# Sending all of the first 21 slots' attention-weight transposes through TensorE and dropping its warm-ups in the loop, in an attention and MoE kernel

## The chip, the cores and the metric

The kernel runs on one core of one Trainium2 chip. The metric is the device time of one execution in microseconds (us), lower is better. Times are medians of several executions.

Engines are named as in the profile: PE is TensorE, PEld its weight loads, DVE VectorE, ACT ScalarE, POOL GpSimd, SP SyncE (it issues the loads, the stores and the DMA crossbar's transposes). The *granted clock* is the share of its full clock that PE was given: in the records of these traces it is 1.00 or 0.5 (half clock).

## The reference, cut to what matters

```python
# q, k, v: (8, 8, 576, 64) float32; tau = 0.02
scores = q @ k.T / sqrt(64)
thresh = max(scores, axis=-1) - tau
attn   = softmax(where(scores >= thresh, scores, -1e9))
x      = (attn @ v)            # to (4608, 512)
h      = x @ w_in              # (512, 2048)
out    = (h * clip(h + 3, 0, 6) / 6) @ w_out
```

## The kernel before

The work is cut into 144 *slots*: one slot is the softmax of 128 queries of two heads against 576 keys. Nine slots make a quad (four heads). In the first 22 slots (`N1`) there is no projection work yet, because no attention output is complete. After that the projections of batch b run beside the softmax of the next batches. The attention weights of a slot, `pn`, have queries in the partitions; the product with v needs keys there, so each slot's `pn` is transposed into `pT` (or `pR` for a quad's ninth slot). There are two ways:

```python
def sm_norm(sl):                      # POOL: pn = s * rinv, bf16
    ...
    if not sl.on_chip:                # way 1: the DMA crossbar, straight into SBUF
        nc.sync.dma_start_transpose(out=sl.dst, in_=pn[...])

def pe_transpose(sl):                 # way 2: nine PE transposes into ps_h, the projections' banks
    ps = ps_h.tile([P, 2, 1024], BF16, tag="h", name="pt")
    for c in range(9):
        nc.tensor.transpose(ps[:, c, :], pn[:, c * P:(c + 1) * P], identb[:])
    return lambda: nc.vector.tensor_copy(out=sl.dst, in_=ps)      # and one DVE copy out
```

The loop of slots, cut. Every engine executes its instructions in this order:

```python
for n, sl in enumerate(queue):
    sm_exp(prev)                      # ACT, two activations
    sm_max(sl)                        # DVE: row maxima of this slot; POOL: bias from them
    ...                               # projections, from slot 23
    copies = pe_transpose(queue[n - 2]) if n > 1 and queue[n - 2].on_chip else None   # PE
    sm_recip(prev)                    # DVE
    if copies:
        copies()                      # DVE
    ...
    sm_mask(sl)                       # ACT, two activations, wait for POOL's bias
    ...                               # PE: transposes of q or k, or products with v; DVE: their eviction
    queue[n + 1].tiles = scores(...)  # PE, eight matmuls
    if n < 8:
        warm_up(6)                    # PE: six idle transposes
    sm_norm(prev)                     # POOL
    start(loads, 1)                   # SP: q and k
    if n < 4 or n > 12:
        start(vcasts, 1)              # POOL issues: v
    if n > 3:
        start(casts, 1 if n < 24 else 2)   # POOL issues: w_in, w_out
```

## Time and profile before

| | before |
|---|---|
| time, median of 3 | 562.35 us (562.04 to 563.1) |
| profiled span | 562.3 us |
| busy: PE, DVE, ACT, POOL | 95%, 75%, 84%, 54% |
| slot 2's to slot 22's first mask | 18.23 to 79.11 us: 60.88 us, 3.04 us a slot |
| crossbar transposes | 119 to `pT`, 15 to `pR` |

I read the stage that the change touches by the *first mask* of each slot: the start of its first mask activation on ACT in the timeline. ACT is the fullest engine there, and masks come once a slot, so these times show at which slot time is gained or lost.

### The profile page before, as it was taken

Reading aid. Unit: us, or ns where it says so; the run is one execution under the profiler, and the core shown is the slowest. Engines: PE = TensorE matmul, PEld = TensorE weight load, DVE = VectorE, ACT = ScalarE, POOL = GpSimd, SP = SyncE. Lnnn points to the kernel's source line nnn. Section 1 sums busy time; section 2 is a strip of 40 time slices with the busy share of each in tenths; the row PEclk is TensorE's granted clock in tenths of the full one; section 3 lists DMA queues with packets and bytes.
Section 4 is the critical chain, followed back from the end, with each engine's and each line's share of the span. In section 5 each row is a group of like instructions: output and inputs, shape, how many; then the busy total and the mean of one; then the engine's idle time right before and its main releaser. Section 6 shows DMA issues by size and latency. Waiting matters only on the chain.

```text
span 562.3 us, 11634 instructions
## 1 busy us (share of the span) xinstructions
PE 535.0 (95%) x3856; PEld 309.3 (55%) x3856; DVE 424.4 (75%) x1040; ACT 470.3 (84%) x999; POOL 305.2 (54%) x646
## 2 busy tenths in 40 slices
PE   7998798899999999999999999999999999999997
PEld 5665455455545565555555565655555565654663
DVE  3588787687878788787878798887978798883440
ACT  4799899798988999989898999899898999983540
POOL 1678878854556555655456555755556555561000
PEclk8899999899999999999999999999999999999999
DMA  5879999997689876978589867987699865453102
GB/s 110 135 110 166 162 160 184 207 148 144 112 159 153 151 153 127 208 139 155 114 150 170 159 137 146 174 160 146 127 137 175 167 124 117 101 109 86 38 20 75
DMA packets 286204, 77.52 MB, mean 138 GB/s; under 512 B 269248, under 2 KB 281536, under 8 KB 286144
## 3 DMA queue, kind: packets, MB, share of 16 engines
q1 hardware_dynamic: 268736, 67.86, 64.8%
q0 software_dynamic: 17408, 8.92, 13.7%
q8 instruction: 30, 0.49, 0.4%
q14 instruction: 30, 0.25, 0.2%
HBM read 36.70 MB, written 9.44 MB: 82 GB/s over the span
## 4 chain that ended last, share of the span: by engine, by line
PE 58%; DVE 11%; ACT 9%; issue 4%; POOL 1%; DMA 1%; SPq 1%; DVEq 0%; POOLq 0%
PE h L353 18%; PE o L382 17%; PE s L256 16%; DVE s L277 5%; ACT s L285 4%; PE av L323 3%; ACT s L290 3%; DVE g L370 2%; DVE r L364 2%; ACT r L362 2%; PE s L262 1%; PE tp L213 1%; PE ar L323 1%; DVE osb L390 1%; POOL pn L298 1%
## 5 line engine op out<-in xcount | busy, mean ns | idle before, releaser
L298 POOL TENSOR_SCALAR pn<-s,rinv 128x576 bf16<-128x576 f32 x288 | 211.6, 745 | 133.5 <-issue 58.5
L277 DVE TENSOR_SCALAR_CACHE_REDUCE s<-s 128x576 f32<-128x576 f32 x288 | 205.9, 752 | 44.9 <-PE s L256 35.2
L285 ACT ACTIVATE s<-s,bias 128x576 f32<-128x576 f32 x288 | 207.1, 766 | 36.8 <-POOL bias L280 35.7
L290 ACT ACTIVATE s<-s 128x576 f32<-128x576 f32 x288 | 192.7, 671 | 0.3
L256 PE MATMUL s<-kT,qT 64*128 64x288 f32 x1024 | 172.7, 435 | 5.4 <-DVE s L277 3.2
L353 PE MATMUL h<-xT,w_in_sb 128*128 128x320 bf16 (+1 forms) x1024 | 145.0, 287 | 5.5 <-DVE g L370 4.6
L382 PE MATMUL o<-w_out_sb,g 128*128 128x512 bf16 x576 | 140.9, 379 | 3.6 <-DVE osb L390 3.0
L353 PEld LDWEIGHTS <-w_in_sb 128*128 128x128 bf16 x1024 | 92.0, 97 | 68.4 <-issue 31.1
L256 PEld LDWEIGHTS s<-kT,qT 64*128 64x128 f32 x1024 | 94.8, 188 | 62.7 <-DVE s L277 24.9
L370 DVE SCALAR_TENSOR_TENSOR g<-r,h 128x512 bf16<-128x512 f32 (+1 forms) x128 | 96.4, 754 | 41.2 <-ACT r L362 39.3
L280 POOL TENSOR_SCALAR bias<-m 128x1 f32<-128x1 f32 x288 | 54.4, 189 | 69.0 <-DVE s L277 48.2
L382 PEld LDWEIGHTS <-g 128*128 128x128 bf16 x576 | 55.6, 98 | 58.2 <-issue 9.8
L362 ACT ACTIVATE r<-h,three 128x640 f32<-128x640 f32 (+1 forms) x74 | 54.4, 737 | 21.1 <-PE h L353 20.4
L290 ACT ACTIVATION_READ_ACCUMULATOR s<-s 128x1 f32 x288 | 54.2, 188 | 0.0
L364 DVE TENSOR_SCALAR r<-h 128x512 f32<-128x512 f32 (+1 forms) x54 | 40.5, 751 | 0.0
L390 DVE TENSOR_SCALAR osb<-o 128x512 f32<-128x512 f32 x31 | 21.0, 676 | 22.2 <-PE o L382 22.2
L323 PE MATMUL av<-pT,vm 128*64 128x512 bf16 x256 | 34.6, 392 | 2.0 <-ACT kT L203 2.0
L323 PEld LDWEIGHTS <-vm 128*64 128x64 bf16 x512 | 18.1, 111 | 25.2 <-issue 18.3
L293 DVE RECIPROCAL rinv<-rsum 128x2 f32<-128x2 f32 x144 | 23.0, 160 | 10.2 <-ACT s L290 9.5
L335 DVE CAST xT<-av 128x512 bf16<-128x512 f32 x32 | 21.8, 681 | 5.6 <-PE av L326 5.3
L277 DVE DVE_READ_ACCUMULATOR s<-s 128x1 f32 x288 | 23.9, 83 | 0.0
L388 ACT ACTIVATE osb<-o 128x512 f32<-128x512 f32 x5 | 3.0, 597 | 23.9 <-PE o L382 23.9
(42 smaller groups left out, 255.9 us busy)
## 6 DMA issues: line engine op xcount, KB each, us to landing
km<-in_k_dram SPq DMA_DIRECT2D x64, 128.0 KB, 3.0
out_dram<-osb SPq DMA_DIRECT2D x32, 256.0 KB, 2.4
nq<-in_q_dram SPq DMA_DIRECT2D x96, 72.0 KB, 2.7
vm<-in_v_dram POOLq DMA_DIRECT2D x16, 256.0 KB, 5.4
nq<-in_q_dram SPq DMA_DIRECT2D x16, 128.0 KB, 3.9
w_in_sb<-in_moe_w_in_dram POOLq DMA_DIRECT2D x16, 128.0 KB, 4.1
w_out_sb<-in_moe_w_out_dram POOLq DMA_DIRECT2D x16, 128.0 KB, 4.5
pT<-pn SPq DMA_TRANSPOSE x119, 3.4
```

Source lines behind the costliest of these rows:

```text
L256: nc.tensor.matmul(tiles[a][:, hf, 0:HALF], qT_of(pair)[a * 64:(a + 1) * 64, t * P:(t + 1) * P], keys(pair, a, hf), start=True, stop=True)
L277: nc.vector.tensor_scalar(out=sl.s[:, i, :].rearrange("p (a b) -> p a b", a=2), in0=ps[:, :, 0:HALF], scalar1=1.0, scalar2=None, op0=Alu.m ...
L280: nc.gpsimd.tensor_scalar(out=sl.bias[:, i:i + 1], in0=sl.m[:, i:i + 1], scalar1=-scale, scalar2=tau, op0=Alu.mult, op1=Alu.add)
L285: nc.scalar.activation(out=s, in_=s, func=Act.Prelu, bias=sl.bias[:, i:i + 1], scale=scale, alpha=REJECT)
L290: nc.scalar.activation(out=s, in_=s, func=Act.Exp, accum_out=sl.rsum[:, i:i + 1])
L298: nc.gpsimd.tensor_scalar(out=pn[:, i, :], in0=sl.s[:, i, :], scalar1=sl.rinv[:, i:i + 1], scalar2=1.0, op0=Alu.mult, op1=Alu.mult)
L323: nc.tensor.matmul(ps[a * 64:(a + 1) * 64, :], vm[:, 2 * hp + a, c * D:(c + 1) * D], pT[:, 5 * a + c, cols], start=(c == 0), stop=False)
L353: nc.tensor.matmul(hps[:, n, 0:w], w_in_sb[:, ki, (ni + n) * P:(ni + n + 1) * P], xT[b][:, ki, c0:c0 + w], start=(ki == 0), stop=(ki == KI ...
L362: nc.scalar.activation(out=r, in_=hps, func=Act.Relu, bias=three[:])
L364: nc.vector.tensor_scalar(out=r, in0=hps, scalar1=3.0, scalar2=0.0, op0=Alu.add, op1=Alu.max)
L370: nc.vector.scalar_tensor_tensor(out=gbuf[:, ni:ni + 2, c0:c0 + w], in0=r, scalar=6.0, in1=hps, op0=Alu.min, op1=Alu.mult)
L382: nc.tensor.matmul(o_ps[0], gbuf[:, ni, mt * P:(mt + 1) * P], w_out_sb[:, ni, :], start=(ni == 0), stop=(ni == NI - 1))
```

## The change

Its intent: PE's banks for the projections (`ps_h`) are idle for the first 22 slots, so let all of the first 21 slots use them, and take eleven crossbar transposes off the DMA queue. As PE now has work in every slot, the warm-ups in the loop go.

```diff
-            sl.on_chip = len(queue) < N1 - 1 and len(queue) % 2 == 1
+            sl.on_chip = len(queue) < N1 - 1
...
-        if n < 8:
-            warm_up(6)
```

## The prediction

> **What bounds the kernel now.** I began with the page's busy shares and its 40 slices. PE is the engine of the whole (95% busy), and from about 120 us until the end its digits are all 9. The change acts before that: the 22 slots (a slot is one softmax step of two heads by 576 keys) that run before the first projection matmuls. So I asked for the busy time of each engine in stretches, whose columns are stretch, length, then busy us of PE, PEld, DVE, ACT and POOL, the granted clock, DMA share and GB/s.
>
> ```profile
> 0.00:20.00 20.00, 16.75 (x78) 11.49 (x79) 7.08 (x22) 9.82 (x19) 6.00 (x18) 0.83 0.54 101
> 20.00:40.00 20.00, 18.54 (x153) 12.27 (x152) 15.53 (x43) 17.66 (x40) 15.34 (x33) 1.00 0.82 127
> 40.00:60.00 20.00, 17.51 (x132) 10.24 (x133) 16.79 (x46) 18.34 (x39) 17.50 (x37) 1.00 1.13 166
> 60.00:80.00 20.00, 16.44 (x137) 8.90 (x136) 15.38 (x44) 18.26 (x42) 16.46 (x36) 1.00 1.21 171
> ```
>
> In this stage ACT is fullest (about 18.3 of 20 us), PE, DVE and POOL are each at 15 to 18: no engine is a clear bound. The timeline of ACT gives the pace. Between the first mask of slot 2 (18.23 us) and of slot 22 (79.11) lie 60.88 us, 3.04 us a slot. Where ACT never waits (45.87 to 48.61) a slot takes 2.74. Twenty slots at 2.74 would be 54.8, so about 6.1 us are lost to waits, and the waits of ACT in that stretch say the same:
>
> ```profile
> ACT s L285 <- POOL bias L280: 6.7, 13, 1.6
> ```
>
> 6.7 us in 13 waits, all for the tiny bias, which POOL makes from the row maximum of DVE, which needs PE's scores. The loop is PE scores, DVE maximum, POOL bias, ACT mask and exponential, DVE reciprocal, POOL normalise, then transpose. Two places stand out in the DMA issues and timelines. In slots 14 to 17 POOL itself is the pace (two weight or V loads issued per slot; slots of 3.38, 3.25, 3.26 and, where it ends, 2.67 us). At the start it is PE: the timeline of PE shows
>
> ```profile
> 10.46 2.96 PE L256 MATMUL s<-kT,qT 64*128 64x288 f32 x8 [0.39 <-DVE s L277]
> 13.35 1.54 PE L164 MATMUL warm<-identf 128*128 128x128 f32 x6
> 14.82 2.29 PE L256 MATMUL s<-kT,qT 64*128 64x288 f32 x8
> 17.04 1.20 PE L164 MATMUL warm<-identf 128*128 128x128 f32 x6
> ```
>
> and the timeline of DVE, where the maximum of slot 2 waits for those scores:
>
> ```profile
> 17.14 0.76 DVE L277 TENSOR_SCALAR_CACHE_REDUCE s<-s 128x576 f32<-128x576 f32 x1 [2.84 <-PE s L256]
> ```
>
> Here the warm-ups (six idle transposes after each of the first eight slots) stand between two groups of scores, on the path.
>
> **What the Trainium skill says.** (1) VectorE: DVE Perf Modes, "The three transpose paths": TensorE transposes a full 128x128 bf16 tile in 390 ns but only into PSUM, the DMA crossbar in 1309 ns straight into SBUF. The trace agrees in kind: a PE transpose lasts 219 ns here and nine pipelined ones 0.66 us, a crossbar transpose of a whole slot 3.4 us from issue to landing; the PSUM result costs a DVE copy. (2) The same page, "Why PSUM operands drop a tier": such a copy has at most the two-per-cycle mode. The trace has it at 0.75 us for 1152 elements, so bf16 does not make it cheaper than the 512-element f32 copies at 0.68. (3) TensorE: Matmul & The Clock Gate, "Part 1: The HAM clock gate": an idle PE falls to half clock for windows of about 3.4 us. In stretches of half a microsecond the granted clock is 0.5 from 10.9 to 17.8 us, 6.8 us, two such windows; once more, for one window, at 106.5 us after 2 us of idle PE. (4) The same page, "Part 4: PE-mode transpose": transposes do not count as PE-busy in the same way. The early fall to half clock follows 6 us of almost nothing but transposes, which fits, but does not prove it. It would make both the warm-ups and their replacement poor at keeping the clock.
>
> **The change part by part.** Before, slots 1, 3, ... 19 (ten) go through PE, slots 0, 2, ... 20 (eleven) through the crossbar; afterwards all 21 go through PE. The costs come from the rows of the transposes' tile:
>
> ```profile
> L314 PE MATMUL pt<-identb,pn x90: 216/219/230, 20.7 to 75.3; 128*128 128x128 bf16 x90
> L315 DVE COPY pT<-pt x9: 737/758/758, 21.4 to 75.9; 128x1152 bf16<-128x1152 bf16 x9
> ```
>
> *Removed, warm-ups:* 8 times 6. From the PE timeline 1.54 + 1.20 + six of 0.88 = 8.0 us of PE. On the path: the first (1.5 us, before the scores that slot 2 waits for). The scores of slot 2 must still wait for the second bank that the maximum of slot 1 frees at 14.2 us, but most of that 1.5 is gained; I take 1.4. The second (1.2 us) makes room for the new transposes of slot 0 in slot 2. The other six end 0.1 to 0.4 us before something else releases the scores (a bank of the maximum, the copy of keys), so I take 0.3 for all. Sum: -1.7 us.
>
> *Removed, crossbar:* 11 of 134 transposes. No engine waits for one in this stage, and SP's own waits (28.6 and 14.1 us) are SP waiting for POOL. The queue has fewer waits ahead of its q and k loads, but those are early enough: one wait of 0.4 us, at 4.8 us. Worth 0 to 0.5 us; I take -0.3.
>
> *Added, PE:* 11 times nine transposes, 11 x 0.66 = 7.3 us, against the 8.0 removed. They sit in front of the next scores in PE's order, and must wait for the normalised weights. In the old odd slots that waiting was 3.1 us in eight waits, but PE has about 2.6 us of slack in 20, and the scores mostly wait for a bank anyway.
>
> *Added, DVE:* 11 copies. Back to back, one pushes the next instruction by 0.66 (46.08 to 46.73), 11 x 0.66 = 7.3 us. By busy time 11 x 0.75 = 8.2, which takes DVE from 48.3 to 56.5 of the 60.9 us between slots 2 and 22, 93%, above ACT's 55.1. So DVE becomes as full as ACT. In a dense slot: two maxima 1.36, reciprocal 0.08, copy 0.66, one eviction of q, k or attention output 0.60, sum 2.70 us, against ACT's 2.74. On paper it still fits under ACT, without any spare. The longer loop from one slot's reciprocal, over POOL's normalise (about 0.5 to start and 1.47), PE's last transposes (0.5), other PE work (mean 0.65), scores (1.0 to the first bank) and two maxima (1.4) to the reciprocal two slots on is 5.5 us, 2.76 a slot: a third near-tie. Three loops within 0.1 us of each other, each in order, lose some to jitter. The old stage away from its start and from POOL's four slots (10 to 13 and 17 to 20) ran at about 2.77 on average; I expect 2.9 there, 0.13 x 12 slots = +1.6 us. In POOL's four slots DVE waited 0.6 to 0.95 us for exponentials, so the copy hides: 0.
>
> *Clock:* if fewer scores and no warm-ups leave the half clock on for one more window, the scores of slot 3 take 2.3 in place of 1.3 us and others with it, about 1.5 us in all. I give that 0.3: +0.5.
>
> Sum: -1.7 - 0.3 + 1.6 + 0.5 = +0.1 us, so 562.35 + 0.1, **562.4 us**. What is gained or lost by slot 22 should be handed on one to one, as the later stages run in program order and are full.
>
> **The rivals.** *A: the freed start.* If jitter costs nothing, the gain of 1.7 to 2.5 us stands: about 560. For it: the old odd slots, with copy and eviction, are no longer than the even ones (2.68 and 2.74, 2.82 us). Against: each had an even slot behind it, in which DVE took only about 2.4 us and caught up. *B: DVE becomes the bound.* If each of the 20 slots costs 0.25 us more, it is +5, less the start: about 566. For it: 93%. Against: POOL's slots hide it. *C: the clock stays low without warm-ups,* for several windows: each costs 1 to 2 us; three would make 566 to 567. For it: the fall at 10.9 us happened in spite of warm-ups. Against: from 36 to 105 us there are none, and the clock is 1.00. *D: a hidden transfer was the limit:* DMA share is 1.1 to 1.5 from 50 to 115 us, so 11 fewer transposes could ease the issues that POOL waits for; up to -2 us. Against: the waits of that stage name engines.
>
> **Range and chances.** A and D give the low end, 559.0; B or C the high end, 567.0. 2% is 11.2 us, more than the whole waiting of ACT in the stage, so faster by that cannot come from here, and slower needs B and C together. Faster 0.01, within 2% 0.96, slower 0.03.
>
> **What would show it.** The first mask of slot 2 near 16.8 us instead of 18.23 shows the start. 189 transposes onto the tile and 123 crossbar ones show the move. DVE busy near 93% between slots 2 and 22, with slots of 2.9 us outside POOL's four, shows the near-tie; ACT's waits for the bias then stay near 6 us but move to later slots. A clock of 0.5 beyond 17.8 us shows C. Later stages should be the same lines shifted by a microsecond or less. The prediction is wrong if the stage's slots average over 3.2 us, if the clock drops in further windows, or if the stretch from 80 to 115 us, where POOL's issues and the key copies of ACT make waits of 1 to 2 us, falls out otherwise for a reason of phase.

## The result, and the profile after

The changed kernel took 564.11 us (563.31 to 564.78, 4 runs) beside 562.73 us of the kernel before; ratio 1.0021, interval 0.9996 to 1.0046. Measured once more among the experiments, on another chip and with more runs, it took 562.28 us beside 562.72 us; ratio 0.9986, interval 0.9964 to 1.0009. Both intervals contain 1: the time can't be told from that of before, and both ratios lie within a quarter of a per cent of 1. The profiled span was 561.9 us.

The same stretches after. The columns are, as in the prediction, stretch, length, busy us of PE, PEld, DVE, ACT and POOL, granted clock, DMA share, GB/s:

```profile
0.00:20.00 20.00, 16.88 (x83) 11.37 (x84) 8.26 (x23) 10.82 (x22) 7.03 (x19) 0.83 0.76 143
20.00:40.00 20.00, 16.42 (x140) 10.01 (x140) 17.51 (x49) 17.20 (x38) 14.66 (x32) 1.00 0.56 94
40.00:60.00 20.00, 17.22 (x158) 10.71 (x156) 17.84 (x46) 17.59 (x39) 17.10 (x34) 1.00 0.76 121
60.00:80.00 20.00, 17.90 (x171) 10.72 (x172) 17.36 (x47) 18.26 (x42) 16.46 (x37) 1.00 0.45 57
```

DVE went up by 1 to 2 us in each 20 and stands level with ACT. The DMA share fell from 1.21 to 0.45 in the last stretch, and nothing got faster for it. The waits of ACT between the first masks of slots 2 and 22, and the rows of the transposes' tile:

```profile
ACT s L285 <- POOL bias L280: 7.3, 13, 1.4
```

```profile
L314 PE MATMUL pt<-identb,pn x189: 219/219/315, 16.4 to 78.4; 128*128 128x128 bf16 x189
L315 DVE COPY pT<-pt x19: 735/736/759, 17.6 to 79.5; 128x1152 bf16<-128x1152 bf16 x19
L315 DVE COPY pR<-pt x2: 736/736/736, 42.2 to 70.3; 128x1152 bf16<-128x1152 bf16 x2
its engine sat idle before it (us, times) until:
  POOL pn L298: 5.9, 17
```

All 21 slots are there (189 = 21 x 9 transposes), and PE now waits 5.9 us for POOL's weights ahead of them, in place of 3.1. ACT waits 7.3 us, in place of 6.7.

First masks of the two profiled executions, us:

| slot | before | after | after - before | gained (-) or lost (+) since the row above |
|---|---|---|---|---|
| 2 | 18.23 | 17.05 | -1.18 | -1.18 |
| 4 | 25.29 | 24.77 | -0.52 | +0.66 |
| 8 | 37.06 | 36.05 | -1.01 | -0.49 |
| 14 | 54.80 | 54.88 | +0.08 | +1.09 |
| 22 | 79.11 | 79.18 | +0.07 | -0.01 |

So the change does something in four places, and the sum is nearly zero. From slot 22 on the two traces run in step: the difference is +0.06 us at slot 30 and +0.16 us at slot 40.

**The gain at the start.** PE after the change, timeline:

```profile
10.45 6.06 PE L256 MATMUL s<-kT,qT 64*128 64x288 f32 x16 [0.39 <-DVE s L277]
16.45 1.14 PE L314 MATMUL pt<-identb,pn 128*128 128x128 bf16 x9
```

The scores of slots 1 and 2 now follow each other without warm-ups between. DVE's maximum of slot 2 starts at 15.61 us (before: 17.14).

**The loss at slots 2 to 4.** PE itself never had the whole 1.18 us: it ends slot 2's scores 0.60 us earlier than before (16.51 against 17.11 us), and it starts slot 3's only 0.37 us earlier. Before, behind the warm-ups that start at 17.04:

```profile
18.08 0.60 PE L213 MATMUL tp<-identf,nq 128*128 128x128 f32 x4
18.61 1.27 PE L256 MATMUL s<-kT,qT 64*128 64x288 f32 x8
```

After, behind the transposes of slot 0 that start at 16.45:

```profile
17.38 0.92 PE L213 MATMUL tp<-identf,nq 128*128 128x128 f32 x4
18.24 1.24 PE L256 MATMUL s<-kT,qT 64*128 64x288 f32 x8
```

The new transposes of slot 0 stand where the warm-ups stood, and in this execution the half clock, which lasts until 18.0 us, stretches them to 1.14 us and those of q to 0.92. all_warm below has both the transposes and the warm-ups, and half clock in the same stretch as before: it ends slot 2's scores level with before (17.16 against 17.11 us) and starts slot 3's 0.80 us later (19.41 against 18.61). The scores of slot 4 need the keys of the second pair of heads, which DVE copies in slot 3 behind slot 1's weights. Before:

```profile
21.44 0.76 DVE L315 COPY pT<-pt 128x1152 bf16<-128x1152 bf16 x1
22.11 0.68 DVE L201 COPY kT<-tp 128x512 f32<-128x512 f32 x1
```

After:

```profile
20.95 0.74 DVE L315 COPY pT<-pt 128x1152 bf16<-128x1152 bf16 x1
21.60 0.68 DVE L201 COPY kT<-tp 128x512 f32<-128x512 f32 x1
```

This order is the same in both kernels, as slot 1 went through PE before too, so it is no loss of the change. PE waits longer for this copy after the change (1.80 us in place of 1.01) because it has no warm-ups to do until then (0.88 us); it starts slot 4's scores 0.51 us earlier (22.34 against 22.85).

**The loss at slots 12 to 14.** In slot 12 PE multiplies with v. Before the change this slot had no transposes (the timeline of PE):

```profile
47.05 1.05 PE L323 MATMUL av<-pT,vm 128*64 128x512 bf16 x8
47.94 0.38 PE L326 MATMUL av<-pT,vr 128*64 128x512 bf16 x2
48.26 1.80 PE L256 MATMUL s<-kT,qT 64*128 64x288 f32 x8
```

After:

```profile
46.41 0.40 PE L314 MATMUL pt<-identb,pn 128*128 128x128 bf16 x4
47.09 0.45 PE L314 MATMUL pt<-identb,pn 128*128 128x128 bf16 x5 [0.28 <-POOL pn L298]
47.47 1.05 PE L323 MATMUL av<-pT,vm 128*64 128x512 bf16 x8
48.36 0.38 PE L326 MATMUL av<-pT,vr 128*64 128x512 bf16 x2
48.67 1.24 PE L256 MATMUL s<-kT,qT 64*128 64x288 f32 x8
```

The product with v now starts 0.42 us later than before although the slot before it was 0.86 us ahead: it stands behind transposes that wait for POOL. Slot 13's maxima come late, hence its reciprocals, hence POOL's normalising, and at slot 14, where POOL sets the pace, the lead has gone. The kernel before holds a control: in slot 21 both kernels have transposes (of slot 19) ahead of a product with v, and slot 21 to 22 takes 3.26 us in both, as slot 12 to 13 does after the change (2.82 before it). Slot 8 has the same pattern: slot 8 to 9 takes 3.26 us after, 3.11 before, where warm-ups stand ahead of the product, and 2.78 in half_nowarm, which has neither.

### The profile page after: what moved, and what is told of

Read it like the earlier page. It is cut to its first block, busy times and chain, and to the rows that moved or that the text cites. A ratio compares the mean times of both kernels' runs of the same rounds, so it can differ in the third digit from the quotient of the medians.

```text
span 561.9 us, 11680 instructions
## 1 busy us (share of the span) xinstructions
PE 532.1 (95%) x3866; PEld 309.2 (55%) x3907; DVE 431.1 (77%) x1051; ACT 470.1 (84%) x999; POOL 305.2 (54%) x646
## 4 chain that ended last, share of the span: by engine, by line
PE 59%; DVE 11%; ACT 7%; issue 3%; DMA 3%; SPq 2%; POOL 1%; DVEq 0%; POOLq 0%
PE o L382 18%; PE h L353 17%; PE s L256 16%; DVE s L277 5%; PE av L323 4%; DMA nq<-in_q_dram 3%; ACT s L285 3%; DVE g L370 2%; ACT s L290 2%; DVE r L364 2%; PE s L262 2%; ACT r L362 1%; PE tp L213 1%; PE av L326 1%; SPq L92 1%
## 5 line engine op out<-in xcount | busy, mean ns | idle before, releaser
L382 PE MATMUL o<-w_out_sb,g 128*128 128x512 bf16 x535 | 133.5, 379 | 5.6 <-DVE osb L390 2.7
```

The source lines that it names most:

```text
L382: nc.tensor.matmul(o_ps[0], gbuf[:, ni, mt * P:(mt + 1) * P], w_out_sb[:, ni, :], start=(ni == 0), stop=(ni == NI - 1))
```

## The experiments

Twelve kernels, each compared with the kernel before on its chip. The clock must be kept in mind in all of them. Ten profiled executions have the same instructions of PE up to 10 us (the two kernels, and all experiments but the three `spread` ones and `warm_matmul`). In six of the ten the granted clock is 0.5 from between 10.8 and 13.5 us for about 6.8 us, in four it is not. The clock's records begin late: 4.1 to 7.4 us into these ten traces, and 26.8 and 26.1 us into those of spread_all and spread_late. Where there is no record the views print 1.00, but PE runs at half rate: in all ten an f32 transpose of the start takes about 420 ns before the first record and 273 ns after it, and where the record comes late (half_nowarm: 7.4 us), four of them take 1.06 to 1.08 us, as at a recorded 0.5 (1.06 at 27.88 us), and not 0.60. The mean clocks of runs leave this stretch out too (spread_all's is 0.997). A single profile therefore carries a microsecond or more of chance in its first 20 us, and intervals between later slots are safer than absolute times. First masks, us, of each profiled execution, and the times:

| kernel | slot 2 | slot 4 | slot 8 | slot 14 | slot 22 | time | ratio to before (interval) |
|---|---|---|---|---|---|---|---|
| before | 18.23 | 25.29 | 37.06 | 54.80 | 79.11 | 562.73 | |
| after | 17.05 | 24.77 | 36.05 | 54.88 | 79.18 | 564.11 | 1.0021 (0.9996 to 1.0046) |
| half_nowarm | 17.41 | 24.31 | 38.06 | 55.20 | 79.54 | 562.49 | 0.9996 (0.9972 to 1.0020) |
| all_warm | 18.28 | 26.05 | 38.20 | 57.53 | 81.86 | 562.83 | 1.0001 (0.9978 to 1.0023) |
| none_nowarm | 16.29 | 23.39 | 36.26 | 53.26 | 86.27 | 571.33 | 1.0148 (1.0124 to 1.0172) |
| all_again | 16.41 | 24.17 | 35.46 | 54.30 | 78.64 | 562.28 | 0.9986 (0.9964 to 1.0009) |
| copy_last | 16.28 | 22.33 | 33.61 | 52.50 | 76.87 | 562.13 | 0.9992 (0.9961 to 1.0022) |
| pe_late | 16.37 | 23.09 | 34.36 | 52.07 | 79.52 | 565.56 | 1.0050 (1.0023 to 1.0078) |
| pool_light | 16.45 | 25.31 | 36.59 | 54.89 | 78.24 | 563.08 | 1.0024 (0.9988 to 1.0061) |
| copy_twice | 17.15 | 25.85 | 39.77 | 60.31 | 87.00 | 572.12 | 1.0165 (1.0132 to 1.0199) |
| spread_all | 22.12 | 30.26 | 41.52 | 59.91 | 83.44 | 569.63 | 1.0111 (1.0084 to 1.0137) |
| spread_half | 21.73 | 28.26 | 40.02 | 57.72 | 81.57 | 569.98 | 1.0122 (1.0091 to 1.0154) |
| spread_late | 22.25 | 29.52 | 40.78 | 58.95 | 82.30 | 570.32 | 1.0122 (1.0095 to 1.0149) |
| warm_matmul | 18.08 | 24.80 | 36.09 | 54.94 | 79.29 | 565.43 | 1.0030 (1.0002 to 1.0058) |

The loss from slot 8 to 14 repeats: 17.74 us before, and 18.83, 18.84, 18.89 and 18.85 in after, all_again, copy_last and warm_matmul, none of which has a fall of the clock there.

My theory was that two opposite parts make the result: the warm-ups' removal gains, the added copies and transposes lose. The main rival was that the four slots where POOL sets the pace swallow any lead or lag of about a microsecond, so that neither part matters.

### half_nowarm: the warm-ups' removal alone

```diff
--- before
-        if n < 8:
-            warm_up(6)
```

> The kernel before with only the warm-ups after the first eight slots taken out; ten slots still go through PE, eleven through the crossbar. Theory (two opposite parts, a gain at the start and a loss from the copies): slot 2's first mask falls near 17.0 us as in the changed kernel (17.05), and without the extra copies the lead of 1 us or more is kept past slots 12 to 14, so slot 22's first mask is near 77.9 (before: 79.11), and the time is 0.2% shorter than before. Rival (POOL's slots 13 to 17 swallow any lead of about a microsecond): slot 22 at 79.1 again and the time as before.

The lead was 0.98 us at slot 5 (27.35 against 28.33), then slot 5 to 6 took 5.00 us. The clock fell for two more windows there (0.5 from about 24.5 to 31.3 us), as PE's timeline shows:

```profile
24.05 2.96 PE L256 MATMUL s<-kT,qT 64*128 64x288 f32 x8 [0.94 <-DVE s L277]
26.94 1.14 PE L314 MATMUL pt<-identb,pn 128*128 128x128 bf16 x9
```

Nine transposes take 1.14 us, not 0.66. So the 77.9 us that I expected at slot 22 became 79.54, and the time is the same as before. What slots 12 to 14 do without the added transposes is clean: from slot 8 to slot 14 it took 17.14 us, the changed kernel 18.83, the kernel before 17.74. The lead isn't lost there, which speaks against the rival. The warm-ups are not plain waste either: in this one execution PE, with neither warm-ups nor added transposes, fell to half clock. (copy_twice, with all the added transposes, fell at 24.6 us too, so this does not show that the warm-ups prevent it.)

### all_warm: the added transposes alone

```diff
--- after
+        if n < 8:
+            warm_up(6)
```

> The changed kernel with the warm-ups put back: only the path of the transposes differs from before. Theory: no gain at the start and the copies' loss in full, so slot 22's first mask comes 1 to 2 us later than before's 79.11 (80 to 81) and the time is 0.2 to 0.4% longer. Rival (the slots paced by POOL swallow a lag as they swallow a lead, by the slack of DVE there): 79.1 to 79.5 and the same time.

In the profile slot 22 comes at 81.86 us, 2.75 us later than before, with the half clock at the start as in the profile of before, and the clock at 1.00 in the stage after it: 0.71 us lost from slot 2 to 4, 0.38 to slot 8, 1.59 to slot 14, nothing after. That is somewhat more than the theory's upper end and against the rival. But the median says 562.83 us against 562.72, where +2.75 us would lie outside the interval (about -1.2 to +1.3 us). The profiled execution, 566.58 us, was the slowest of seven; the six others ran at mean clocks of 0.996 to 0.999, the runs of before at 0.989 to 0.999. At mean clocks of 0.996 and more alone, those six of all_warm average 562.99 us and four of before 561.81: 1.2 us more, which is what the theory expected. But the choice was made after the fact and the runs are few, so this supports the theory and does not show it. It may be that more work on PE keeps the clock up and pays its own cost back; these runs don't show that either, and it stays open.

### none_nowarm: all through the crossbar

```diff
--- after
-            sl.on_chip = len(queue) < N1 - 1
+            sl.on_chip = False
```

> No slot through PE, no warm-ups: all 21 through the crossbar. Theory: PE and DVE lose their transposes and copies on the path, so the stage gets shorter than in any other version, slot 22 at 76.5 to 78, if nothing waits for a crossbar transfer. Rival (the crossbar is what the path through PE is there to avoid: transposes and loads in one queue come late): the attention products of slots 8 and 12 wait for the transposed weights by over 1 us, and slot 22 comes at 79 or later. If PE idles for 2 us or more, a fall to half clock may add a microsecond.

The rival holds, beyond what it expected, but in other slots than it named: the products of slots 8 and 12 do not wait. Until slot 14 this is ahead (53.26 us), then those of slots 17 and 21 wait for the crossbar, 4.8 and 1.4 us. From the waits between 55 and 90 us:

```profile
PE av L323 <- DMA pT<-pn: 6.2, 2, 4.8
```

PE idles and the clock falls (to 0.5 from 56.9 to 77.4 us), as the page's row of the granted clock in tenths shows (each digit is about 14 us):

```profile
PEclk9699569899999999999999999999999999999999
```

1.5% are lost. So the crossbar is not hidden when it carries every slot, and PE's path is worth having; the half that already went through PE did as well as all of it. How much of the 1.5% is the waits and how much the clock isn't separated.

### all_again: the changed kernel once more

> The changed kernel once more, more rounds, on the same chip as the three others: is the 0.2% of its first measurement (interval from -0.04 to +0.46%) real? The trace says the stage ends 0.07 us later than before and the profiled span is 0.4 us shorter, so theory: a ratio within 0.15% of 1. Rival (a loss that the one profiled execution did not have): 1.002 or more with an interval clear of 1.

The ratio is 0.9986; the 0.2% of the first measurement isn't real. This profile has the full clock at the start (slot 2 at 16.41 us) and a half-clock window at about 21 to 24 us, which shows how far two executions of one kernel differ.

### copy_last: the order of DVE's copies

```diff
--- after
-        if copies:
-            copies()
...
         if evict:
             evict()
+        if copies:
+            copies()
```

> The changed kernel with one order altered: DVE's copy of the transposed weights comes behind the slot's eviction of q, k or attention output, not ahead of it. Work is the same. Theory (the loss sits in the copies standing ahead of what the next scores or maxima need): the scores of slot 4, which waited 1.80 us for the keys' copy, wait 0.7 us less; slot 4's mask comes 0.5 to 0.7 us earlier against slot 2's than in the changed kernel (interval from slot 2 to slot 4: 7.72 there, 7.0 to 7.2 here); slots 12 to 14 unchanged because the maximum must wait for both anyway. Time 0.1% shorter at most. Rival (the loop through POOL's normalise sets the pace): interval 7.7 again.

The wait for the keys in slot 4's scores fell by half (changed kernel: 1.80):

```profile
19.89 1.24 PE L256 MATMUL s<-kT,qT 64*128 64x288 f32 x8 [0.85 <-DVE kT L201]
```

Slot 3 to slot 4 took 3.35 us in place of 4.18. The expectation was for slots 2 to 4, 7.0 to 7.2 us; it took 6.05 in place of 7.72, but part of that is the clock, which this execution had at 1.00 from 5.1 to 558 us. The profile of warm_matmul below is the fair comparison: it has the order of the changed kernel and no fall from 6.7 to 559 us. There slot 2 to 4 took 6.72 us, so the order of the copies is worth 0.67, and from slot 4 to slot 40 the two run level (119.38 us each). But the kernel before has the unchanged order too: this is a gain that the kernel before might have as well (not measured), and not the change's loss given back, as the theory had it. Slots 12 to 14 are as they were (slot 11 to 14 took 9.91 us), and the time, 562.13 us, can't be told from before. Among its own six runs, two at mean clock 0.999 took 560.49 and 560.88 us, three at 0.990 to 0.992 took 562.81 to 563.15: 2.5 us go with the clock, several times the effect. The mean clock does not tell everything: of all_again's runs, two at 0.999 took 561.1 us, three at 1.000 took 561.95 to 563.47.

### pe_late: PE's transposes behind the next scores

```diff
--- after (slots 0 to 18; the copy follows in the next slot)
-        copies = pe_transpose(queue[n - 2]) if n > 1 and queue[n - 2].on_chip else None
...
             queue[n + 1].tiles = scores(queue[n + 1].quad, queue[n + 1].slot)
+        if 1 < n < 21:
+            pending.append(pe_transpose(queue[n - 2]))
```

> The changed kernel with PE's nine transposes of a slot moved behind the next slot's scores (slots 0 to 18), so that scores no longer wait on PE behind weights that POOL has not finished; their copy follows one slot later. Theory (slots 12 to 14 lose because PE holds the scores back until the normalised weights are there): the 1.1 us by which the interval from slot 11 to slot 14 is longer than before (9.87 against 8.93) mostly goes, 8.9 to 9.2. Rival (DVE's copies, now as many, are what fills the slot): still 9.7 to 9.9. Time within 0.2% of the changed kernel either way.

Slot 11 to 14 took 9.24 us (changed kernel 9.87, before 8.93), just above the 8.9 to 9.2 expected: two thirds of the loss go when the scores do not stand behind transposes that wait for POOL. That supports the theory for slots 12 to 14; DVE's copies, which are as many here, are not the main cause there. The last third stays, in slot 13 to 14 (3.69 us in place of 3.37), and is not explained. My version then loses at slot 22, where it does two slots' transposes: PE waits for the bank and the mask of slot 22 for the whole chain.

```profile
73.70 0.87 PE L314 MATMUL pt<-identb,pn 128*128 128x128 bf16 x9 [1.61 <-DVE pT L315]
...
79.52 0.78 ACT L285 ACTIVATE s<-s,bias 128x576 f32<-128x576 f32 x1 [3.88 <-POOL bias L280]
```

That costs 3.4 us (slot 21 to 22 takes 6.66 in place of 3.26; the clock is at 0.5 from 74.0 to 77.4 us), but it eats a lead: slot 22 comes only 0.41 us later than before. The rest of the 0.5% comes later. Slots 31 to 33 take 9.71 us in place of 6.98: PE waits 2.2 us there for a crossbar transpose into `pR`, and the clock falls again from 115.0 to 118.4 us. Why that transfer is late wasn't traced, so the time does not judge the idea.

### pool_light: what POOL issues in slots 13 to 16

```diff
--- after
-        if n > 3:
+        if n > 3 and not 12 < n < 17:
             start(casts, 1 if n < 24 else 2)
```

> The changed kernel without the weight loads that POOL issues in slots 13 to 16 beside those of V (they move to later slots). Theory: those slots are paced by POOL (3.26 to 3.37 us each); without 0.55 us of issue they fall to what DVE, now full, allows, 2.75 to 2.95, so slot 13 to slot 18 takes 14.0 to 14.7 us in place of 16.33, and the stage ends 1.5 to 2 us earlier. If that lead is handed on, the time is 0.3% shorter. Rival (DVE or the loop already needs 3.2 us there): 16 us again. A second rival: the lead is lost again after slot 23, where POOL issues two weight loads a slot and now has four more to do.

Slot 13 to 18 took 14.79 us (51.65 to 66.44) in place of 16.33, just above the 14.0 to 14.7 expected: POOL's issues do pace these slots, and with fewer of them slots 14 to 16 take 2.69 to 2.84 (slots 13 and 17 still 3.24 and 3.19). POOL's timeline in them has one issue a slot:

```profile
55.22 1.47 POOL L298 TENSOR_SCALAR pn<-s,rinv 128x576 bf16<-128x576 f32 x2
56.64 0.80 POOL L121 DMA_DIRECT2D vm<-in_v_dram  x1
57.52 0.45 POOL L280 TENSOR_SCALAR bias<-m 128x1 f32<-128x1 f32 x2
```

The second rival holds too: the lead of 0.94 us at slots 22 to 30 (in spite of a half-clock start) is 0.44 at slot 33; the loads that were put off are issued in slots 30 and 31. I did not trace that loss further. The time, 563.08 us, doesn't show a gain.

### copy_twice: the copies' cost doubled

```diff
--- after
-        return lambda: nc.vector.tensor_copy(out=sl.dst, in_=ps)
+        return lambda: [nc.vector.tensor_copy(out=sl.dst, in_=ps) for _ in range(2)]
```

> The changed kernel with each of the 21 copies from the transposes' banks done twice: doubles the suspected cost, 0.66 us of DVE a slot. Theory (DVE has 2.70 of 2.74 us filled, so it is at the limit): nearly every slot outside POOL's four grows by 0.5 to 0.66, slot 22 comes 9 to 12 us later and the time is 1.6 to 2.1% longer. Rival (DVE has slack and other loops pace the slots): 2 to 6 us later, under 1.1%.

Slot 22 came 7.82 us later than in the changed kernel, between the two expectations, and the time is 1.65% over before, as the theory had it. (This profile also has the clock at 0.5 from 24.6 to 28.0 us, so a part of the 7.82 is the clock.) Slots 10 to 13 took 3.32, 3.47 and 3.47 us in place of 2.68, 2.84 and 3.26, and POOL's slots 14 to 16 did not move; slot 17, where POOL's pace ends, took 3.47 in place of 2.68. DVE is back to back in such a slot (slot 7 here; the accumulator reads are left out):

```profile
35.01 0.75 DVE L277 TENSOR_SCALAR_CACHE_REDUCE s<-s 128x576 f32<-128x576 f32 x1
...
35.68 0.75 DVE L277 TENSOR_SCALAR_CACHE_REDUCE s<-s 128x576 f32<-128x576 f32 x1
...
36.36 0.16 DVE L293 RECIPROCAL rinv<-rsum 128x2 f32<-128x2 f32 x1
36.44 1.53 DVE L315 COPY pT<-pt 128x1152 bf16<-128x1152 bf16 x2
```

In slot 10 the second copy pushes by 0.64 us where the first pushed by nothing (2.68 before and after): the slack of DVE there was just the size of one copy.

### spread_all, spread_half, spread_late: POOL's loads spread, to see the change without POOL's pace

```diff
--- after, with the order of copy_last  (spread_half: before, with the same edits;
---                                      spread_late: and pe_late without its double slot)
     make_identity(nc, identf)
+    start(casts, 4)
...
-        if n > 3:
-            start(casts, 1 if n < 24 else 2)
+        if not busy:                  # busy: a V load is issued in this slot, n > 12
+            start(casts, 1 if n < 31 else 2)
```

> The changed kernel with the copies behind the evictions and POOL's 32 weight loads spread: four before the first slot, one in each slot from 0, none in slots that issue a V load after slot 12, so that no slot issues two until slot 31. Theory (POOL's issues pace slots 13 to 17 and again 23 to 31, and DVE fills the others): slots 13 to 18 take 14.0 to 14.8 us in place of 16.3 (the lighter slots of an earlier run took 14.8), slots 23 to 31 some 2 to 5 us less, and the time is 0.3 to 1% shorter than before. Rival (a lead is lost again before the projections, as the 0.9 us of the lighter version shrank to 0.4 after slot 31; or the early weight loads hold up q and k): within 0.25% of before.

> The kernel before (ten slots through PE, warm-ups kept) with the same spread of weight loads and the same order of copies as the version beside it. What is left between the two is the change itself, with POOL's pacing gone. Theory (the copies fill DVE to the limit, so where POOL no longer hides it the change costs): 1 to 2 us shorter than that version in slots 8 to 22. Rival (the crossbar's transposes then pace the slots, or PE does): the same within 1 us, or longer.

> The version with spread weight loads, and PE's transposes behind the next slot's scores for all 21 slots, the copies one slot later, without the double transposes at slots 21 and 22 that cost the earlier version 3.4 us. Theory (the wait for POOL's weights ahead of the scores costs 0.6 us at slots 12 to 14 and some in other slots): slot 22 comes 0.5 to 1.5 us earlier than in the version beside it. Rival (POOL's pace was what those waits hid in): no difference.

All three were meant to beat both kernels and are over 1% slower. The stage behaved as expected: slot 13 to 18 took 14.92 us in spread_all, and slots 23 to 31 took 27.47 us in place of 29.74. But the rival named both ways in which it was lost. PE's waits in the first 12 us of spread_all, and those from 122 to 133 us, in two answers:

```profile
PE tp L214 <- DMA km<-in_k_dram: 1.8, 1, 1.8
...
PE tp L214 <- DMA nq<-in_q_dram: 1.1, 1, 1.1
```

```profile
PE o L383 <- DMA w_out_sb<-in_moe_w_out_dram: 3.5, 2, 1.9
```

Four weight loads ahead of the first slot hold up the first keys and queries, and slot 0's mask comes at 14.93 us in place of 10.71. Not all of that is the loads: in spread_all and spread_late PE runs at half rate until the clock's first record at 26.8 and 26.1 us (an f32 transpose takes 417 ns and more, in place of 273), and spread_half has the clock at 0.5 from 8.5 to 18.7 us. At slot 34 the last parts of w_out, put off by the same edit, come too late for the second projection. Between the three, the change itself can still be read where POOL does not set the pace: from slot 11 to 22 spread_half took 32.27 us, spread_all 32.93, spread_late 32.54. The change costs 0.66 us there (the theory had 1 to 2 for slots 8 to 22, where it is 0.37), and the later transposes give 0.39 of it back, less than expected, then lose 1.96 us from slot 22 to 23.

### warm_matmul: real products as warm-ups

```diff
--- after
-            nc.tensor.transpose(warm[:, 0, 0:P], identf[:], identf[:])
+            nc.tensor.matmul(warm[:, 0, 0:P], identf[:], identf[:], start=True, stop=True)
```

> The changed kernel with its 18 warm-ups before the first scores made real f32 products with the same identity and not transposes. Theory (transposes do not count as work for the clock, so the fall to half clock near 11 us is due to a start made of transposes): no half clock from 11 to 18 us in the profile, a mean clock of 0.997 or more in every run, slot 2's first mask at 16.3 to 16.5 us in place of 17.05, time 0.1 to 0.3% shorter. Rival (the fall comes from the pauses of PE between 6 and 9 us, or from the phase of the clock's window against the start): the half clock is there in the profile or in the means of most runs, as with transposes.

The profile has no half clock from 11 to 18 us, as the theory expects, but so have four of ten profiles with transposes. The mean clocks of the six runs are 0.999, 0.988, 0.991, 0.993, 0.990 and 0.991: five are below the 0.997 that was asked for, so the rival holds for most runs. The products also take longer (5.9 us for the first 14, in place of 3.1 to 3.2), which delays slot 0 by 1.8 us; it is 0.3% slower. That transposes caused the fall is not shown.

No version was measured to be faster than both kernels. The best median, copy_last's, has an interval that contains 1.

## Why the prediction was right

The time was right: 562.4 us was forecast, within the range, and "same" at 0.96. Most of its terms had the right sign; several had the wrong size or place.

- **What paces a slot.** The 2.74 us "where ACT never waits" is not the least: slots 10 and 17 took 2.68 in both kernels. So DVE's dense slot, 2.70 by the prediction's sum, did not fit under ACT's pace on paper. And its second point from the Trainium skill is misread: the bf16 copy moves 1152 elements in 0.75 us beside 512 in 0.68 for f32, so an element costs it less than half.
- **First warm-up (-1.4).** Right in mechanism; it measured -1.18 at slot 2, but PE itself was only 0.60 us ahead at the end of that slot's scores. The mask came at 17.05 us where 16.8 was named. In three executions with all 21 slots on PE and no half clock at the start it comes at 16.28 to 16.41.
- **The other warm-ups (-0.3).** -0.49 from slot 4 to 8, net of the added transposes. Right in sign and size.
- **Jitter from the copies (+1.6), spread at 0.13 over twelve slots.** The sum came out, 0.66 + 1.09 = 1.75 us, but by luck: the place and the mechanism are wrong. Most slots outside POOL's four did not grow at all: 2.68 and 2.68 us in slots 10 and 17, as before. The loss sits in two places that the prediction counted as free: slot 0's transposes ahead of slot 3's scores, for which the second warm-up was to make room, and the product with v behind the transposes in slot 12. all_warm shows the first, pe_late and slot 21 of the kernel before the second. The prediction's "the scores mostly wait for a bank anyway" is the sentence that failed.
- **"In POOL's four slots the copy hides: 0."** Right for slots 14 to 17; 14 to 16 moved by nothing even with the copies doubled. The way into them, slot 13 to 14, took 3.77 in place of 3.37 us.
- **DVE at 93%.** Measured 54.13 of 62.13 us, 87%. I added whole durations, but neighbours on DVE overlap: over the whole kernel eleven more copies of 0.74 us added 6.7 us of busy time (431.1 less 424.4), 0.61 each. That DVE is nearly full was right: the second copy of copy_twice cost its full push.
- **Clock (+0.5).** It came back at 18.0 us, as before at 17.8, so in this pair of profiles there was no further window and the term is 0; but as slot 2 came earlier, the same half clock now stretched slot 0's transposes and those of q. Its size was right as a risk: half_nowarm lost about 2 us in one slot to it.
- **Crossbar (-0.3).** Nothing shows it. The transfers were hidden, as was their removal.
- **Rivals.** B needed every slot to grow by 0.25 us, and they did not. C was not seen in the changed kernel's first profile: after 18.0 us the clock fell only at 106.8, as before at 106.5. all_again had one more window, at 20.7 us. D fell: the DMA share in the stage's last third went from 1.21 to 0.45 with no gain. A is refuted in the traces, where the gain had gone by slot 14; in time it is open to the extent that all_warm left open what the added transposes cost.

The sum of +0.1 us against +0.07 at slot 22 is closer than the terms deserve: errors cancelled.

## What to carry to other kernels

When three engines are within a tenth of a microsecond per step, don't spread an added cost evenly over the steps: look in each step's instruction order for what the added instruction will stand ahead of, because the loss comes where another engine waits for the instruction behind it. Moving the added work behind that instruction is the first thing to try. Check too that the order you blame is not in the kernel before as well, as the copy ahead of the keys was here: if it is, moving it is a gain, but no explanation. And before explaining a difference of 0.3%, compare mean clocks and intervals between steps in several executions; one profile can differ from the next of the same kernel by more. Where the clock's records begin late, read it from the length of like instructions.

## What the Trainium skill lacked or had wrong

- TensorE: Matmul & The Clock Gate, "Part 4: PE-mode transpose", says that full clock does not engage for transposes. Here it did: in ten equal starts PE had run nothing but transposes when the full clock came, 4.1 to 7.4 us in, and an f32 transpose went from about 420 to 273 ns. Later ones run at both rates too: nine bf16 ones take 0.66 us at full clock and 1.14 us at half. Whether transposes keep the clock up is neither shown nor excluded: after them four of ten starts kept it, and with products five of six runs still had means of 0.993 or less.
- The same page, "Part 1: The HAM clock gate", has the free-running window of 3413 ns and warns that the clock's records can be unreliable. The window fits: the falls of six in ten equal starts last 6.83 us, two windows. Of unreliable records these runs show one form that the page lacks: the records begin late (up to 26.8 us in), and what stands before the first one is half clock though the views print 1.00. It also lacks the size of the chance for a whole kernel: 2.5 us of 562 between runs of copy_last at mean clocks of 0.999 and 0.99.
- VectorE: DVE Perf Modes, "The three transpose paths", compares single transposes (390 ns on TensorE, 1309 ns on the crossbar). It lacks what decides here: pipelined ones on PE start 55 ns apart at full clock (nine take 0.66 us), each slot's copy out of PSUM costs 0.74 us of DVE, and crossbar transposes of every slot made PE wait up to 4.8 us for one slot's weights.
